# Second layer in f16 pairs instead of fp32r, scaled per tile from the energy of its tokens

## The chip, the core and the metric

The kernel runs on one core of one Trainium2 chip. The core has five engines with a queue of their own each: TensorE (PE, the matrix engine; PEld is its loading of the stationary matrix), VectorE (DVE), ScalarE (ACT), GpSimd (POOL) and SyncE (SP, which issues the transfers). The metric is the device time of one execution in microseconds; lower is better.

## What is computed

The input x has 8 batches of 3072 tokens with 256 numbers. Two layers follow a Fourier transform:

```python
X = np.fft.fft(np.fft.fft(x, axis=1), axis=2).real       # x: 8 x 3072 x 256
h = np.maximum(np.maximum(X @ w1, X @ w2), X @ w3)       # 256 -> 768
y = h @ w_out                                            # 768 -> 256, first layer's output
h = y @ w_in                                             # 256 -> 1024, second layer
e = np.exp(h - h.max(-1)); sm = e / (e.sum(-1) + 1e-09)
solu = h * sm
ln = (solu - mean(solu)) / np.sqrt(var(solu) + 1e-06) * g_ln
out = ln @ w_out2                                        # 1024 -> 256
```

The weights of the matrices come as f64 words and are decoded on the chip.

## The kernel before, in words

The work is cut into 48 tiles of 512 tokens, six for each batch. Precision comes from pairs: a number is held as a high and a low part, and a product of two such matrices is three matmuls (high by high, high by low, low by high). Everywhere but in the second layer's first product the parts are f16, brought into range by factors of two.

A batch begins with its loads (`x_load`, line 331), butterflies on POOL (`x_fly`, line 364), the split into f16 parts (`x_norm`, `x_hi`, `x_lo`, the tile `uh`), and the first half of the transform (`alpha_mm`, line 393). The stretch of the program in which a batch's 192 alpha matmuls lie between the tiles of the batch before it is called the alpha stretch below; there are seven of them inside the stream. A transpose by DMA gives `z` (`z_tr`), and `beta_mm` (line 428) finishes the transform for one tile, as the pair `pq`.

For each tile, the first layer takes 14 products `l1_mm` (line 529, two of them with `w3l`), each evacuated by ACT (`l1_b`, line 301) and DVE (`l1_n`, `l1_c`, lines 549, 562 and 563), six `relu` (line 568), six splits (`r_hi` on ACT, `r_lo` on POOL, lines 572 and 577) and six `m_mm` (line 587). `m_add` (DVE, line 591) gives the layer's output in two halves of 128 x 512. ACT rounds each half to fp32r (`mo_hi`, line 596) and POOL takes the rest (`mo_lo`, line 600); the pair `mo` is the second layer's input.

The second layer goes by four blocks of 128 tokens to a tile. `h_mm` (line 649) is 12 matmuls of 512 columns with blocks of `mo` as the stationary and the fp32r pair `win` as the moving matrix, in a PSUM tile `h` of which there is one. DVE takes the maximum (`h_max`, line 658) and three small operations on one column (`h_q`, lines 661 to 664), ACT the exponential (`h_exp`, line 671), DVE the product `v` (`h_v`, line 677), which frees `h`. ACT squares `v` (line 682) and rounds it to f16 (`v_hi`, line 704), POOL does small column operations (lines 687 to 699) and the low part (`v_lo`, line 708), the pair is transposed by DMA, and `o_mm` (line 722) is 24 matmuls of 256 columns.

The order on every engine is fixed when the program is built: a list scheduler (`Schedule.run`) keeps a model of each engine's clock from written durations, and takes on each engine the operation whose rank is lowest. The rank rests on a due time in tiles, to which a table of numbers, `BIAS`, adds by kind of operation. `CAPACITY` says how many buffers a pool has. Two PSUM banks (`misc`) are shared by alpha, beta, `o_mm` and the small sums over partitions (`spread`, line 320, a fp32 matmul with a 128 x 128 matrix of ones as the stationary, which stands in the trace as two matmul records).

Of the kernel before, what the change touches and what calls it, by code (L numbers as in the profile page):

```python
# [1158 lines left out]
```

## Time and profile before

| | |
|---|---|
| median of 3 runs | 2186.63 us (2185.48 to 2187.26) |
| profiled execution | 2187.91 us, of which its span, from the first to the last instruction, is 2186.1 us |
| mean granted TensorE clock | 0.983 of full speed |
| busy share of the span | PE 94%, PEld 72%, DVE 85%, ACT 65%, POOL 66% |
| the chain that ended last | PE 75%, DVE 11%, issue 4%, ACT 4%, POOL 3%, DMA 2% |
| of it, by line | h L649 21%, omm L722 19%, l L529 17%, m L587 14% |

Busy time is the time in which an engine had an instruction in work. The chain is followed back from the last instruction, at each step to what released it. A share over the whole span is an average of stretches with different limits.

### The profile page before, as it was taken

To read this page: it belongs to the slowest core of one execution; us is meant where nothing else is said; L and a number is where in the kernel's file an instruction comes from. 1 tells how busy PE (TensorE), PEld (TensorE's weight loads), DVE (VectorE), ACT (ScalarE), POOL (GpSimd) and SP (SyncE) were. 2 spreads that over 40 slices of the span, in tenths; PEclk is the share of its full clock that TensorE was granted. 3 is DMA by queue.
4 is the path that set the end of the run, shared out by engine and by line. 5 is a ranking of instruction groups with operands and counts; after the bars stand their busy time and mean duration, and the time that the engine had idled before them with its cause. 6 is when DMAs were issued, how large, how long until landed. Compare 5 with 4: busy or idle time off the path is not lost.

```text
span 2186.1 us, 44046 instructions
## 1 busy us (share of the span) xinstructions
PE 2044.8 (94%) x16130; PEld 1575.9 (72%) x16130; DVE 1849.0 (85%) x3993; ACT 1430.0 (65%) x2680; POOL 1434.7 (66%) x1688
## 2 busy tenths in 40 slices
PE   3568999999999999999999999999999999999998
PEld 2445777777777777777777777777777777777776
DVE  7978888888888888987898888988899888888884
ACT  2656765686657865677666776668666786666655
POOL 3657855686657855588566876579556885555653
PEclk8689999999999999999999999999999999999999
DMA  8352344744456344744348344553437543443324
GB/s 249 117 114 55 82 78 88 159 83 83 83 116 136 73 86 79 157 101 77 73 80 167 88 83 83 117 130 78 92 59 163 108 78 74 77 84 75 71 59 106
DMA packets 532617, 216.61 MB, mean 99 GB/s; under 512 B 504368, under 2 KB 504496, under 8 KB 532272
## 3 DMA queue, kind: packets, MB, share of 16 engines
q1 hardware_dynamic: 532400, 213.80, 47.0%
q8 instruction: 126, 2.06, 0.4%
q14 instruction: 91, 0.75, 0.1%
HBM read 62.76 MB, written 25.17 MB: 40 GB/s over the span
## 4 chain that ended last, share of the span: by engine, by line
PE 75%; DVE 11%; issue 4%; ACT 4%; POOL 3%; DMA 2%; SPq 0%; POOLq 0%; ACTq 0%; DVEq 0%
PE h L649 21%; PE omm L722 19%; PE l L529 17%; PE m L587 14%; PE alpha L393 2%; PE beta L428 1%; DVE sv L568 1%; DVE l L549 1%; DVE v L677 1%; POOL rhl L577 1%; DMA vt<-vh 1%; POOL mo L600 1%; POOL vh L708 1%; ACT bs L301 1%; DMA xa<-in_x_dram 1%
## 5 line engine op out<-in xcount | busy, mean ns | idle before, releaser
L649 PE MATMUL h<-win,mo 128*128 128x512 f32 x2280 | 577.5, 402 | 7.9 <-DVE v L677 7.9
L722 PE MATMUL omm<-wf,vt 128*128 128x256 f16 x4608 | 535.8, 273 | 11.4 <-DVE x L406 4.4
L722 PEld LDWEIGHTS <-vt 128*128 128x128 f16 x4608 | 450.5, 98 | 88.4 <-issue 10.0
L649 PEld LDWEIGHTS h<-win,mo 128*128 128x128 f32 x2280 | 418.4, 189 | 97.8 <-PE l L529 5.3
L529 PE MATMUL l<-pq,wl 128*128 128x256 f16 (+2 forms) x3456 | 455.8, 273 | 30.0 <-DVE sv L568 11.5
L708 POOL TENSOR_TENSOR vh<-v,vh 128x1024 f16<-128x1024 f32 x188 | 403.1, 2144 | 63.8 <-ACT vh L704 59.4
L549 DVE SCALAR_TENSOR_TENSOR l<-ny,wn,l 128x256 f32<-128x256 f32 (+1 forms) x672 | 322.5, 484 | 144.4 <-ACT bs L301 136.4
L577 POOL TENSOR_TENSOR rhl<-sv,rhl 128x512 f16<-128x512 f32 x288 | 335.7, 1169 | 161.2 <-ACT rhl L572 159.8
L587 PE MATMUL m<-rhl,wo 128*128 128x512 f16 x1728 | 415.7, 379 | 15.0 <-DVE s L591 10.6
L529 PEld LDWEIGHTS <-wl 128*128 128x128 f16 x3456 | 321.7, 97 | 130.3 <-issue 45.9
L301 ACT ACTIVATE bs<-l 128x256 f32<-128x256 f32 (+1 forms) x576 | 216.1, 381 | 161.3 <-PE l L529 157.1
L682 ACT ACTIVATE jk<-v,hst 128x1024 f16<-128x1024 f32 x192 | 220.1, 1147 | 144.9 <-DVE v L677 144.7
L658 DVE TENSOR_REDUCE hst<-h 128x1 f32<-128x1024 f32 x190 | 232.0, 1221 | 74.5 <-PE h L649 72.9
L587 PEld LDWEIGHTS <-wo 128*128 128x128 f16 x1728 | 163.9, 98 | 167.5 <-DVE s L591 11.3
L572 ACT CAST rhl<-sv 128x512 f16<-128x512 f32 x288 | 177.3, 616 | 152.2 <-DVE sv L568 136.1
L677 DVE SCALAR_TENSOR_TENSOR v<-h,hst,e 128x1024 f32<-128x1024 f32 x190 | 242.7, 1278 | 7.2 <-ACT e L671 5.0
L671 ACT ACTIVATE e<-h,hst 128x1024 f32<-128x1024 f32 x190 | 211.6, 1114 | 54.5 <-DVE hst L658 52.1
L695 POOL TENSOR_SCALAR hst<-hst,sc 128x1 f32<-128x1 f32 x192 | 66.0, 344 | 219.4 <-ACT jk L682 190.9
L704 ACT CAST vh<-v 128x1024 f16<-128x1024 f32 x192 | 200.0, 1042 | 4.2 <-DMA vt<-vh 2.7
L364 POOL TENSOR_TENSOR uv<-xs 96x512 f32<-96x512 f32 x128 | 167.7, 1334 | 32.9 <-DMA xs<-in_x_dram 25.3
L568 DVE SCALAR_TENSOR_TENSOR sv<-l,sv 128x512 f32<-128x512 f32 x240 | 164.8, 687 | 2.9
L600 POOL TENSOR_TENSOR mo<-s,mo 128x512 fp32r<-128x512 f32 x96 | 123.2, 1292 | 54.8 <-ACT mo L596 54.3
(148 smaller groups left out, 2558.9 us busy)
## 6 DMA issues: line engine op xcount, KB each, us to landing
xs<-in_x_dram SPq DMA_DIRECT2D x120, 384.0 KB, 4.1
out_dram<-ob SPq DMA_DIRECT2D x96, 256.0 KB, 2.9
raw<-in_w_dram SPq DMA_DIRECT2D x6, 768.0 KB, 5.3
raw<-in_w_out_dram SPq DMA_DIRECT2D x14, 256.0 KB, 2.9
xa<-in_x_dram SPq DMA_DIRECT2D x8, 384.0 KB, 7.9
vt<-vh SPq DMA_TRANSPOSE x192, 4.3
raw<-in_w_in_dram SPq DMA_DIRECT2D x4, 512.0 KB, 3.8
cb<-in_c_beta_dram SPq DMA_DIRECT2D x1, 1536.5 KB, 10.8
```

Source lines behind the costliest of these rows:

```text
L301: act.activation(dst, src, AF.Copy, scale=scale)
L529: mm(o, w_[w], hl[:, a, e, c0:c0 + n_], start=(n == 0), stop=(n == 2))
L549: dve.scalar_tensor_tensor(p[:, 0:WA], pq[s][1][:, 0:WA], w, p[:, 0:WA], ALU.mult, ALU.add)
L577: pool.tensor_tensor(t[:, 1], svs.pop((s, j, 0)), t[:, 0], ALU.subtract)
L587: mm(m[:, h], wo[:, w, j, hs], t[:, a], start=(j == 0 and n == 0), stop=(j == NJF - 1 and n == 2))
L649: mm(hp[:, f], m[:, a, d, ts_], win[:, w, d, fs], start=(n == 0), stop=(n == 5))
L658: dve.tensor_reduce(st[:, 0], y["h"], op=ALU.max, axis=AX.XY, negate=True)
L671: act.activation(y["e"], y["h"], AF.Exp, bias=st[:, 0], scale=1.0, accum_out=st[:, 3])
L677: dve.scalar_tensor_tensor(y["v"], y["h"], st[:, 2], y["e"], ALU.mult, ALU.mult, accum_out=st[:, 4])
L682: act.activation(new(hpool[0], "jk", [128, 2, 512], F16), y["v"], AF.Square, bias=st[:, 4], scale=-float(FF2), accum_out=st[:, 6])
L708: engine.tensor_tensor(y["vh"][:, 1], y["v"].rearrange("p a b -> p (a b)"), y["vh"][:, 0], ALU.subtract)
L722: mm(y["o"][:, 0:D], vt[:, a * 8 + c], wf[:, w, c], start=(n == 0), stop=(n == 23))
```

## The change

The second layer's input and its first matrix become f16 pairs. For that the values must be brought into f16's range, which the change does by a scale for each tile, taken from the energy of the tile's tokens: ACT squares the high half of `z` and sums it (`z_square`), one fp32 matmul of one column sums over the partitions (`z_total`), three small DVE operations make a power of two and its reciprocal (`z_least`, `z_root`, `z_recip`), and four on POOL give the scales that later steps take as a column (`z_unit`, `z_true`, `z_eps`). `mo_hi` becomes two ACT operations for each half: the f16 high part, and that part scaled back to f32 in a tile `mw`, from which POOL takes the low part. `win` holds three parts (high, low, and the high part scaled by 2**-11 for the product with the low part of `mo`), and its loading phase measures its maximum, scales it and splits it. `h_exp` scales the negated maximum by an ACT operation on one column and then scales inside the exponential; the first small operation of `h_q` takes a column in place of the number 1.0. All numbers of `BIAS` are new, several written durations too, `xa` has three buffers instead of four and `wi` four instead of one.

```diff
-CAPACITY = dict(l1=2, m=1, h=1, misc=2, xs=2, uv=2, uh=2, z=2, pq=2, bs=3, sv=3, sw=1, s2=2, rhl=3, mo=2, hst=4, e=1, v=2,
-                vh=2, vt=3, ob=2, xb=2, dg=1, raw=2, xa=4, wr=3, wi=1)
+CAPACITY = dict(l1=2, m=1, h=1, misc=2, xs=2, uv=2, uh=2, z=2, pq=2, bs=3, sv=3, sw=1, s2=2, rhl=3, mo=2, hst=4, ms=5, mw=2, e=1, v=2,
+                vh=2, vt=3, ob=2, xb=2, dg=1, raw=2, xa=3, wr=3, wi=4)
 X_POOL = ((0, 1, 0, 1, 0, 1, 0, 1), (1, 1, 1, 1, 1, 1, 1, 1))
...
-BIAS = {("ah", 0): -35.57, ("ah", 1): -76.89, ("al", 0): -26.93, ("al", 1): -159.58, ("alo", 0): -2.02,
+BIAS = {("xla", 0): -199.12, ("xmax", 0): -74.211, ("xld", 0): 91.084, ("xfly", 0): 125.294, ("xhs", 0): 51.043,
...
-    win = wp.tile([128, 2, 2, FF2], F32R, name="win")
+    win = wp.tile([128, 3, 2, FF2], F16, name="win")
...
-    def m_unit(b):
-        dve.tensor_scalar(xbt[b][:, 12:13], xbt[b][:, 10:11], sc[:, SC_M:SC_M + 1], 4.0, ALU.mult, ALU.mult)
+    m_unit = [
+        (130, lambda b: dve.tensor_scalar(xbt[b][:, 12:13], xbt[b][:, 10:11], sc[:, SC_M:SC_M + 1], 4.0, ALU.mult, ALU.mult)),
+        (130, lambda b: dve.tensor_scalar(xbt[b][:, 12:13], xbt[b][:, 12:13], am[:, 23:24], None, ALU.mult)),
+        (78, lambda b: dve.reciprocal(xbt[b][:, 13:14], xbt[b][:, 12:13])),
+    ]
...
+    mst, msp = {}, {}
+    MS_V, MS_R, MS_U, MS_T, MS_I, MS_E, MS_S = range(7)
+    def ms_col(s, c):
+        return mst[s][:, c:c + 1]
+    def z_square(s):
+        mst[s] = new(lp, "ms", [128, 8], F32)
+        act.activation(new(fp, "zj", [128, 8, 128], F16), zt[s][:, 0:8], AF.Square, scale=2.0**-8, accum_out=ms_col(s, MS_S))
+    def z_total(s):
+        msp[s] = misc("total")
+        mm(msp[s][:, 0:1], unit, ms_col(s, MS_S))
+    def z_least(s):
+        dve.tensor_scalar(ms_col(s, MS_V), msp.pop(s)[:, 0:1], 2.0**-20, None, ALU.max)
+    def z_root(s):
+        v = ms_col(s, MS_V).bitcast(I32)
+        dve.tensor_scalar(v, v, 1, 0x7F800000, ALU.logical_shift_right, ALU.bitwise_and)
+    def z_recip(s):
+        dve.reciprocal(ms_col(s, MS_R), ms_col(s, MS_V))
+    def z_unit(s):
+        pool.tensor_scalar(ms_col(s, MS_U), ms_col(s, MS_R), 2.0**-32, 2.0**-33, ALU.mult, ALU.mult)
+    def z_true(s):
+        t = xbt[s // NSB]
+        pool.tensor_scalar(ms_col(s, MS_T), ms_col(s, MS_V), t[:, 12:13], 2.0**76, ALU.mult, ALU.mult)
+        pool.tensor_scalar(ms_col(s, MS_I), ms_col(s, MS_R), t[:, 13:14], 2.0**-76, ALU.mult, ALU.mult)
+    def z_eps(s):
+        pool.tensor_scalar(ms_col(s, MS_E), ms_col(s, MS_I), sc[:, SC_E:SC_E + 1], ms_col(s, MS_I), ALU.mult, ALU.mult)
...
-            op(("be", *k), "PE", (360, 720)[p], beta_mm, k, v, deps=[("zt", s), ("constb",), *before], take=["misc"],
-               give=["z"] if p else [])
-            op(("bh", *k), "ACT", (264, 530)[p], beta_hi, k, v, deps=[("be", *k)] + [("bh", s, 0)] * p,
-               take=[] if p else ["pq"])
+            op(("be", *k), "PE", (360, 720)[p], beta_mm, k, v, deps=[("zt", s), ("constb",), *before],
+               take=["misc"] if p else ["misc", "pq"])
+            op(("bh", *k), "ACT", (264, 530)[p], beta_hi, k, v, deps=[("be", *k)] + [("bh", s, 0)] * p)
             op(("bl", *k), "DVE", 350, beta_lo, k, v, deps=[("bh", *k)], give=["misc"])
+        op(("zs", s), "ACT", 1135, z_square, (s,), v, deps=[("zt", s)], take=["ms"])
+        op(("zr", s), "ACT", 0, lambda s: zt.pop(s), (s,), v, deps=[("zs", s), ("be", s, 1)], give=["z"])
+        op(("ze", s), "PE", 120, z_total, (s,), v, deps=[("zs", s)], take=["misc"])
+        sch.chain(("zv", s), "DVE", [(130, z_least), (130, z_root), (78, z_recip)], (s,), v, deps=[("ze", s)], give=["misc"])
+        op(("zu", s), "Pool", 330, z_unit, (s,), v, deps=[("zv", s)])
+        op(("zm", s), "Pool", 760, z_true, (s,), v + 0.5, deps=[("zv", s), ("mu", b)])
+        op(("zq", s), "Pool", 390, z_eps, (s,), v + 1, deps=[("zm", s), ("wfc",)])
...
-        return 2.0**-21 if i < 2 else xbt[s // NSB][:, 12:13]
+        return 2.0**-21 if i < 2 else ms_col(s, MS_U)
...
-            mo[s] = new(hpool[0], "mo", [128, 2, 2, 512], F32R)
-        act.copy(mo[s][:, 0, h], svs[s, h, 2])
+            mo[s] = new(hpool[0], "mo", [128, 2, 2, 512], F16)
+        split_hi(mo[s][:, 0, h], svs[s, h, 2], 2.0**-11)
+        mw[s, h] = new(hpool[0], "mw", [128, 512], F32)
+        split_hi(mw[s, h], mo[s][:, 0, h], 2.0**11)
     def mo_lo(s, h):
         t = mo[s]
-        pool.tensor_tensor(t[:, 1, h], svs.pop((s, h, 2)), t[:, 0, h].bitcast(F32), ALU.subtract)
+        pool.tensor_tensor(t[:, 1, h], svs.pop((s, h, 2)), mw.pop((s, h)), ALU.subtract)
...
-               give=["m", "pq"] + (["xb"] if is_special(s) else []) if h else [])
-            op(("mh", *k), "ACT", 520, mo_hi, k, v, deps=[("ma", *k), ("open",)] + [("mh", s, 0)] * h,
-               take=[] if h else ["mo"])
-            op(("ml", *k), "Pool", 1225, mo_lo, k, v, deps=[("mh", *k)], give=["s2"])
+               give=["m", "pq"] if h else [])
+            op(("mh", *k), "ACT", 1050, mo_hi, k, v, deps=[("ma", *k), ("open",)] + [("mh", s, 0)] * h,
+               take=["mw"] if h else ["mo", "mw"])
+            op(("ml", *k), "Pool", 1225, mo_lo, k, v, deps=[("mh", *k)], give=["s2", "mw"])
...
-                for a, w in ((0, 0), (0, 1), (1, 0)):
+                for a, w in ((0, 0), (0, 1), (1, 2)):
...
-        (72, lambda s, t: dve.tensor_scalar(hx[s, t]["st"][:, 1], hx[s, t]["st"][:, 0], -1.0, 1.0, ALU.mult, ALU.max)),
+        (72, lambda s, t: dve.tensor_scalar(hx[s, t]["st"][:, 1], hx[s, t]["st"][:, 0], -1.0, ms_col(s, MS_I),
+                                           ALU.mult, ALU.max)),
...
-        act.activation(y["e"], y["h"], AF.Exp, bias=st[:, 0], scale=1.0, accum_out=st[:, 3])
+        act.activation(st[:, 11], st[:, 0], AF.Copy, scale=ms_col(s, MS_T))
+        act.activation(y["e"], y["h"], AF.Exp, bias=st[:, 11], scale=ms_col(s, MS_T), accum_out=st[:, 3])
...
-        pool.tensor_scalar(st[:, 8], st[:, 7], sc[:, SC_E:SC_E + 1], st[:, 7], ALU.mult, ALU.mult)
+        pool.tensor_scalar(st[:, 8], st[:, 7], ms_col(s, MS_E), st[:, 7], ALU.mult, ALU.mult)
...
-            sch.chain(("hk", *k), "DVE", h_q, k, v, deps=[("hm", *k)])
-            op(("he", *k), "ACT", 1095, h_exp, k, v, deps=[("hm", *k)], take=["e"])
+            sch.chain(("hk", *k), "DVE", h_q, k, v, deps=[("hm", *k), ("zm", s)])
+            op(("he", *k), "ACT", 1320, h_exp, k, v, deps=[("hm", *k), ("zm", s)], take=["e"])
...
-            sch.chain(("hs", *k), "Pool", [(200, h_g), (270, h_g2), (270, h_var)], k, v + 0.2, deps=[("hq", *k), ("wf",)])
+            sch.chain(("hs", *k), "Pool", [(320, h_g), (390, h_g2), (390, h_var)], k, v + 0.2, deps=[("hq", *k), ("zq", s)])
             if t % 2:
-                op(("hf", s, t // 2), "Pool", 640, h_pow, (s, t // 2), v, deps=[("hs", s, t - 1), ("hs", s, t)])
+                op(("hf", s, t // 2), "Pool", 640, h_pow, (s, t // 2), v, deps=[("hs", s, u) for u in range(t + 1)],
+                   give=["ms"] + (["xb"] if is_special(s) else []) if t == 3 else [])
...
+    def win_norm(h, f):
+        split_hi(tmp["i", h, f], tmp["i", h, f], sc[:, SC_I:SC_I + 1])
     def win_hi(h, f):
-        act.copy(win[:, 0, h, f * 512:(f + 1) * 512], tmp["i", h, f])
+        fs = slice(f * 512, (f + 1) * 512)
+        act.copy(win[:, 0, h, fs], tmp["i", h, f])
+        split_hi(win[:, 2, h, fs], win[:, 0, h, fs], 2.0**-11)
     def win_lo(h, f):
         fs = slice(f * 512, (f + 1) * 512)
-        pool.tensor_tensor(win[:, 1, h, fs], tmp.pop(("i", h, f)), win[:, 0, h, fs].bitcast(F32), ALU.subtract)
+        pool.tensor_tensor(win[:, 1, h, fs], tmp.pop(("i", h, f)), win[:, 0, h, fs], ALU.subtract)
+    def win_join():
+        dve.tensor_reduce(am[:, 22:23], am[:, 24:28], op=ALU.max, axis=AX.X)
     for h in range(2):
         for f in range(2):
             k = ("i", h, f)
             v = -0.3 + 0.1 * (2 * h + f)
             from_f64(k, [w_in2[h * 128:(h + 1) * 128, f * 512:(f + 1) * 512]], wi_dst(k), 512, v, take=["wi"])
-            pop(("wih", h, f), "ACT", 520, win_hi, (h, f), v, deps=[("gd", *k)])
+            pop(("ami", h, f), "ACT", 620, bound, (24 + 2 * h + f, lambda k=k: tmp[k], win[:, 0, h, f * 512:(f + 1) * 512]), v,
+                deps=[("gd", *k)])
+            pop(("wio", h, f), "ACT", 520, win_norm, (h, f), v, deps=[("isc",)])
+            pop(("wih", h, f), "ACT", 1000, win_hi, (h, f), v, deps=[("wio", h, f)])
             pop(("wil", h, f), "Pool", 1225, win_lo, (h, f), v, deps=[("wih", h, f)], give=["wi"])
+    pop(("amij",), "DVE", 80, win_join, (), 0.0, deps=[("ami", h, f) for h in range(2) for f in range(2)])
+    pow2_scale("is", 22, 1, [("amij",)], 0.0)
+    pop(("isc",), "DVE", 135, lambda: recip(SC_I, 23), (), 0.0, deps=[("is", "pow")])
```

The order of instructions, as the built programs have it, at three places.

On PE, in the stream, the end of a block of `h_mm` before; `wl` is the first layer's matrix, `l` its PSUM tile, and an fp32r matmul stands without a weight load of its own in this listing:

```order
L529 LDWEIGHTS wl_74
L529 MATMUL l_13754<-pq,wl_74 128x256
L649 MATMUL h<-win,mo 128x512 x12
L529 LDWEIGHTS wl_74
L529 MATMUL l_13789<-pq,wl_74 128x256
```

and now:

```order
L692 LDWEIGHTS mo
L692 MATMUL h<-win,mo 128x512
L570 LDWEIGHTS wl_74
L570 MATMUL l_7172<-pq,wl_74 128x255
L570 LDWEIGHTS wl_74
```

The block of twelve matmuls stands among the same neighbours as before; its form is that of the f16 products. The added sum over partitions stands once for each of the 48 tiles between such blocks:

```order
L570 LDWEIGHTS wl_74
L570 MATMUL l_7182<-pq,wl_74 128x257
L425 MATMUL total<-ms,unit 128x1
L628 LDWEIGHTS wo
L628 MATMUL m<-rhl,wo 128x512
```

On ACT, around the second layer's input of one tile, before (`bs` is the first layer's evacuation, `ob` the output's, `e`, `jk` and `vh` are the exponential, the square and the rounding of a block, `x` an evacuation of alpha):

```order
L301 ACTIVATE bs<-l_9456 128x256
L301 ACTIVATE bs<-l_9467 128x256
L671 ACTIVATE e,hst<-h,hst 128x1024
L596 CAST mo<-s_9020 128x512
L596 CAST mo<-s_9157 128x512
L729 ACTIVATE ob<-omm,hst 128x256
L402 CAST x_85<-alpha 128x6x16x4
L682 ACTIVATE jk,hst<-v,hst 128x1024
L704 CAST vh<-v 128x1024
```

and now, at a tile's input in the same part of the stream:

```order
L297 ACTIVATE bs<-l_9702 128x256
L715 ACTIVATE hst<-hst,ms 128x1
L716 ACTIVATE e,hst<-h,hst,ms 128x1024
L613 CAST rhl<-sv 128x512
L297 ACTIVATE mo<-s_9277 128x512
L297 ACTIVATE mw<-mo 128x512
L774 ACTIVATE ob<-omm,hst 128x256
L727 ACTIVATE jk,hst<-v,hst 128x1024
L297 ACTIVATE mo<-s_9405 128x512
L297 ACTIVATE mw<-mo 128x512
```

Each half of the input now takes two ACT operations, and each exponential has an operation on one column ahead of it.

On POOL, where a tile's scales are made, now (`ms` is the tile's column of scales, `bs` two cleared columns):

```order
L438 TENSOR_SCALAR ms<-ms 128x1
L442 TENSOR_SCALAR ms<-ms,xb 128x1
L443 TENSOR_SCALAR ms<-ms,xb 128x1
L446 TENSOR_SCALAR ms<-ms,sc 128x1
L732 TENSOR_SCALAR hst<-hst 128x1
L736 TENSOR_SCALAR hst<-hst,ms 128x1
```

The first four are new. Counted in the same listing from the last `vh` of one tile to the last `vh` of the second tile after it, in an alpha stretch, POOL has before 14 `uv`, 7 `uh`, 13 `rhl`, 4 `mo` and 8 `vh`; now it has 16 `uv`, 7 `uh`, 12 `rhl`, 4 `mo`, 8 `vh` and 8 `ms`.

## Rows read from the trace of the kernel before

**Rows 1.** The page: span, and busy time, share and instructions by engine.

```profile
span 2186.1 us, 44046 instructions
...
PE 2044.8 (94%) x16130; PEld 1575.9 (72%) x16130; DVE 1849.0 (85%) x3993; ACT 1430.0 (65%) x2680; POOL 1434.7 (66%) x1688
```

**Rows 2.** Busy time by stretch: opening, ramp, stream, end; then clock and DMA.

```profile
0.00:123.00 123.00, 56.78 (x371) 43.66 (x372) 98.64 (x137) 56.70 (x94) 58.31 (x42) 0.77 0.62 180
123.00:200.00 77.00, 56.92 (x396) 38.78 (x394) 59.79 (x137) 43.66 (x81) 47.84 (x44) 0.90 0.41 86
200.00:2150.00 1950.00, 1903.44 (x15185) 1471.57 (x15184) 1674.02 (x3692) 1313.52 (x2481) 1321.21 (x1588) 1.00 0.47 94
2150.00:2186.00 36.00, 27.66 (x187) 21.85 (x185) 16.59 (x28) 16.07 (x27) 7.38 (x15) 0.95 0.47 103
```

**Rows 3.** Waits of PE from 200 us: total us, times, longest.

```profile
PE m L587 <- DVE s L591: 10.6, 6, 1.8
...
PE alpha L393 <- DVE pq L304: 0.6, 1, 0.6
```

**Rows 4.** Timeline of PE: start, length, operation and count.

```profile
1009.79 3.01 PE L649 MATMUL h<-win,mo 128*128 128x512 f32 x12
1012.64 1.49 PE L529 MATMUL l<-pq,wl 128*128 128x256 f16 x12
...
1034.05 2.75 PE L587 MATMUL m<-rhl,wo 128*128 128x512 f16 x12
1036.64 0.82 PE L529 MATMUL l<-pq,w3l 128*128 128x256 f16 x6
```

**Rows 5.** Groups by line and shape on PE: busy us, mean ns, idle before.

```profile
L649 PE MATMUL h<-win,mo 128*128 128x512 f32 x2280 | 577.5, 402 | 7.9 <-DVE v L677 7.9
...
L649 PEld LDWEIGHTS h<-win,mo 128*128 128x128 f32 x2280 | 418.4, 189 | 97.8 <-PE l L529 5.3 <-issue 4.9
L587 PE MATMUL m<-rhl,wo 128*128 128x512 f16 x1728 | 415.7, 379 | 15.0 <-DVE s L591 10.6 <-POOL rhl L577 4.4
```

**Rows 6.** Timeline of PE around a fp32 sum over partitions.

```profile
413.77 0.39 PE L320 MATMUL spread<-dg,unit 128*128 128x128 f32 x2
413.99 0.82 PE L529 MATMUL l<-pq,wl 128*128 128x256 f16 x6
```

**Rows 7.** The same groups on DVE, small operations.

```profile
L662 DVE TENSOR_SCALAR hst<-hst 128x1 f32<-128x1 f32 x192 | 39.5, 206 | 0.9
...
L664 DVE RECIPROCAL hst<-hst 128x1 f32<-128x1 f32 x192 | 30.1, 157 | 2.5
...
L661 DVE TENSOR_SCALAR hst<-hst 128x1 f32<-128x1 f32 x192 | 28.5, 149 | 0.7
```

**Rows 8.** On ACT.

```profile
L682 ACT ACTIVATE jk<-v,hst 128x1024 f16<-128x1024 f32 x192 | 220.1, 1147 | 144.9 <-DVE v L677 144.7
...
L596 ACT CAST mo<-s 128x512 fp32r<-128x512 f32 x96 | 58.3, 614 | 19.8 <-DVE s L591 19.7
...
L682 ACT ACTIVATION_READ_ACCUMULATOR jk<-v,hst 128x1 f32 x192 | 36.2, 188 | 0.0
...
L853 ACT COPY wn<-prep 128x6 f32<-128x6 f32 x2 | 0.3, 138 | 0.0
```

**Rows 9.** On POOL.

```profile
L577 POOL TENSOR_TENSOR rhl<-sv,rhl 128x512 f16<-128x512 f32 x288 | 335.7, 1169 | 161.2 <-ACT rhl L572 159.8
...
L364 POOL TENSOR_TENSOR uv<-xs 96x512 f32<-96x512 f32 x128 | 167.7, 1334 | 32.9 <-DMA xs<-in_x_dram 25.3 <-DVE uh L304 4.4 <-ACT uh L372 2.3
...
L600 POOL TENSOR_TENSOR mo<-s,mo 128x512 fp32r<-128x512 f32 x96 | 123.2, 1292 | 54.8 <-ACT mo L596 54.3
...
L691 POOL TENSOR_SCALAR hst<-hst,sc 128x1 f32<-128x1 f32 x192 | 68.0, 354 | 19.2
```

**Rows 10.** Two tiles of an alpha stretch, cut at the last vh of each.

```profile
1194.50:1235.80 41.30, 41.30 (x335) 31.75 (x334) 34.57 (x80) 30.63 (x57) 33.62 (x35) 1.00 0.49 106
1235.80:1283.00 47.20, 45.57 (x440) 36.48 (x440) 41.40 (x91) 39.42 (x70) 45.37 (x41) 1.00 0.33 74
```

More of the change, by code (lines that the diff above doesn't have):

```diff
@@ L291, in fft_moe_solu_kernel @@
     x1 = fp.tile([128, NSB, 4, 4, 128], F16, name="x1")
-    SC_W, SC_O, SC_3, SC_F, SC_M, SC_E, SC_V = 0, 1, 2, 3, 8, 9, 10
+    SC_W, SC_O, SC_3, SC_F, SC_I, SC_M, SC_E, SC_V = 0, 1, 2, 3, 4, 8, 9, 10
     def at_least(dst, src, scale=2.0**-13):
@@ L439, in beta_mm @@
             run(WB, 1, 0, 0, lambda t: t[:, 0:1].broadcast_to([128, 128]))
-            zt.pop(s)
         bps[s, part] = p
@@ L466, in fft_moe_solu_kernel @@
             buf = "xs" if b else "xa"
-            op(("xla", *k), "SP", 1090, x_load, k if b else (*k, tp, "xa"), v - 0.5,
+            op(("xla", *k), "SP", 1450, x_load, k if b else (*k, tp, "xa"), v - 0.5,
                deps=[("xla", b, c - 1)] if c else [("xld", b - 1, NCH - 1)] if b else [], take=[buf] if c else [buf, "xb"], lag=2500)
@@ L473, in fft_moe_solu_kernel @@
             v = max(NSB * b - 1.8, -1.0) + 0.09 * c
-            op(("xld", *k), "SP", 1090, x_load, k, v - 0.5, deps=[("xld", b, c - 1)] if c else [("xla", b, NCH - 1)] if b else [], take=["xs"],
+            op(("xld", *k), "SP", 1450, x_load, k, v - 0.5, deps=[("xld", b, c - 1)] if c else [("xla", b, NCH - 1)] if b else [], take=["xs"],
                lag=2500)
@@ L495, in fft_moe_solu_kernel @@
         sch.chain(("xsc", b), "DVE", x_scale, (b,), v, deps=[("xall", b)], give=["misc"])
-        op(("mu", b), "DVE", 130, m_unit, (b,), v + 0.3, deps=[("xsc", b), ("scm",)])
+        sch.chain(("mu", b), "DVE", m_unit, (b,), v + 0.3, deps=[("xsc", b), ("scm",), ("isc",)])
     for s in range(NT):
@@ L506, in fft_moe_solu_kernel @@
             before = [("be", s, 0)] if p else [("be", s - 1, 1)] if s else []
-            op(("be", *k), "PE", (360, 720)[p], beta_mm, k, v, deps=[("zt", s), ("constb",), *before], take=["misc"],
-               give=["z"] if p else [])
-            op(("bh", *k), "ACT", (264, 530)[p], beta_hi, k, v, deps=[("be", *k)] + [("bh", s, 0)] * p,
-               take=[] if p else ["pq"])
+            op(("be", *k), "PE", (360, 720)[p], beta_mm, k, v, deps=[("zt", s), ("constb",), *before],
+               take=["misc"] if p else ["misc", "pq"])
+            op(("bh", *k), "ACT", (264, 530)[p], beta_hi, k, v, deps=[("be", *k)] + [("bh", s, 0)] * p)
             op(("bl", *k), "DVE", 350, beta_lo, k, v, deps=[("bh", *k)], give=["misc"])
-    l1s, svs, rs, rhl, mt, mts, mo = {}, {}, {}, {}, {}, {}, {}
+        op(("zs", s), "ACT", 1135, z_square, (s,), v, deps=[("zt", s)], take=["ms"])
[5 more added lines that the diff above has]
+        op(("zq", s), "Pool", 390, z_eps, (s,), v + 1, deps=[("zm", s), ("wfc",)])
+    l1s, svs, rs, rhl, mt, mts, mo, mw = {}, {}, {}, {}, {}, {}, {}, {}
     def l1_weights(i, j):
@@ L606, in l1_ops @@
         if stays(k[0], k[2]):
-            op(("l1c", *k), "DVE", 790, l1_c, k, v, deps=[("l1n", *k)], give=["bs"])
+            op(("l1c", *k), "DVE", 808, l1_c, k, v, deps=[("l1n", *k)], give=["bs"])
         else:
-            op(("l1c", *k), "DVE", 790, l1_c, k, v, deps=[("l1n", *k)], take=[sv_tag(k[2])], give=["bs", "l1"])
+            op(("l1c", *k), "DVE", 662 if k[2] < 2 else 790, l1_c, k, v, deps=[("l1n", *k)], take=[sv_tag(k[2])], give=["bs", "l1"])
     for s in range(NT):
@@ L617, in fft_moe_solu_kernel @@
             v = s + (2 * j + 1) / 12
-            op(("rl", *k), "DVE", 663, relu, k, v, deps=[("l1c", s, j, 1), ("l1c", s, j, 0)], give=["l1" if stays(s, 1) else "sw"])
+            op(("rl", *k), "DVE", 608, relu, k, v, deps=[("l1c", s, j, 1), ("l1c", s, j, 0)], give=["l1" if stays(s, 1) else "sw"])
             op(("rh", *k), "ACT", 520, r_hi, k, v, deps=[("rl", *k)], take=["rhl"])
@@ L624, in fft_moe_solu_kernel @@
             k = (s, h, 2)
-            l1_ops(k, s + (h + 4.5) / 6, [("w3l",), ("mu", s // NSB)])
+            l1_ops(k, s + (h + 4.5) / 6, [("w3l",), ("zu", s)])
             k = (s, h)
@@ L817, in from_f64 @@
     def from_f64(key, srcs, dst, n, v, take=(), after=()):
-        pop(("ld", *key), "SP", 2.8 * n, f64_load, (key, srcs, n), v - 0.2, deps=after, take=["raw", *take], lag=2000)
+        pop(("ld", *key), "SP", 3.6 * n, f64_load, (key, srcs, n), v - 0.2, deps=after, take=["raw", *take], lag=2000)
         magnitude, parts = f64_parts(key, dst, n)
@@ L853, in w_evac_n @@
         act.copy(wn[:, i - 1], tmp.pop(("n", i))[:, 0:NJF])
-    am = tp.tile([128, 24], F32, name="am")
+    am = wp.tile([128, 28], F32, name="am")
     def amax(col, t):
```

51 lines of the change are left out of this document (24 added, 27 removed), and 57 rows, old and new, of the table BIAS.

## The prediction

> **What bounds the kernel now.** The page comes first: a span of 2186.1 us, PE busy for 2044.8 of it, DVE for 1849.0, ACT and POOL near 1430 [rows 1]. The busy share by stretch says where PE is not busy [rows 2]. In the opening (to 123 us) and the ramp (to 200 us) it idles for 86.3 us; in the stream, from 200 to 2150 us, it is busy for 1903.44 of 1950 us at a granted clock of 1.00, its upper level of 2.4 GHz; the end leaves 8.3 us idle. So in nine tenths of the time PE lacks 46.6 us to being full. What it still waits for is nearly all DVE: the waits of PE after 200 us hold ten lines with DVE as the releaser, from 10.6 us down to 0.6 us [rows 3], together 41.4 us (10.6 + 6.4 + 4.8 + 4.4 + 4.2 + 3.8 + 2.7 + 2.0 + 1.9 + 0.6). Time taken off PE's instructions in the stream is time off the kernel, as far as DVE, ACT and POOL can follow; they are busy there for 86%, 67% and 68%.
>
> **The block h_mm.** In the timeline one block of twelve fp32r matmuls starts at 1009.79 us and its successor at 1012.64: 2.85 us, 237 ns for each matmul. Twelve f16 matmuls of the same 512 columns, `m_mm`, start at 1034.05 and are followed at 1036.64: 2.59 us, 216 ns each [rows 4]. The lengths of single records agree: 402 ns against 379 [rows 5], and 23 ns by the 2304 matmuls (192 blocks of twelve) is 53 us. The form changes, the number and the columns don't. I take the timeline: 192 x 0.26 = 49.9 us less on PE, with 53 us as the other end. The rows show one thing that goes with the longer step: an fp32r weight load lasts 189 ns [rows 5].
>
> The Trainium skill ("TensorE: Matmul & The Clock Gate", section "Back-to-back issue gap") gives a gap at the full clock that depends on the columns alone, about 216 ns for 512. The f16 row meets that and the fp32r row is 21 ns above it; if the rule held for fp32r too, this term would be zero and the sum below 2208 us. The measurement decides here, and the term stays.
>
> **The sum over partitions.** 48 fp32 matmuls of one column come in, each two records. The nearest row is a `spread` of 128 columns in the stream: it starts at 413.77 us and the next matmul at 413.99 [rows 6], 0.22 us with its weight loads. 48 x 0.22 = 10.6 us on PE. Fewer columns can only make it cheaper, but the weight loads remain, so 5 to 11 us; I take 10.6. It waits for `z_square` on ACT, which needs only the transposed `z`, as the beta matmuls do. It also holds one of the two `misc` banks until three small DVE operations are through; alpha, beta and `o_mm` are queued for these banks. That goes into the waits below.
>
> **DVE.** In `h_q` a number becomes a column. The operation with a number takes 149 ns, the one with a column 206 [rows 7]: 192 x 57 ns = 10.9 us. The chain of a tile is three operations like 149 to 206, 149 and 157 ns, about 0.49 us, 23.5 us for 48. Together 34 us, of which the stream gets some 33. None of it lies on PE's path by itself; it takes DVE's slack. DVE is free for 276 of 1950 us now, 14.1%. Afterwards it has 1674 + 33 = 1707 us of work in 1950 - 49.9 + 10.6 + 11 = 1922 us, 11.2% free. I let PE's 41.4 us of waits for DVE grow as this free share falls: 41.4 x (14.1 / 11.2) = 52, **11 us more**. That is a choice; its bounds are 20 us less (the table of priorities is new and may order the stream better: half of the present waits gone) and 40 us more (PE's idle time in the stream nearly doubled).
>
> **ACT.** Each tile gets `z_square`, like the square of 128 x 1024 with its read of the sum, 1147 + 188 ns; two more operations of 128 x 512, 614 ns each; and four operations on one column, of which the nearest rows are 138 ns and, as the upper end, 188 [rows 8]. That is 1.34 + 1.23 + about 0.7 = 3.3 us a tile, 157 us in all. ACT goes from 67% of the stream to about 76%. It hides as long as the order leaves room. On the way of one block, `h` is held 0.14 to 0.19 us longer by the new operation before the exponential, and its matmuls give back 0.26; on the way from `m_add` to the next tile's first block there is 0.61 us more, covered by first-layer matmuls that stand between.
>
> **POOL.** Four column operations a tile like 354 ns [rows 9], 1.4 us; `mo_lo` now writes f16, as `rhl` does, 1169 ns instead of 1292, 0.25 us back. Net 1.2 us a tile, 55 us in all; 68% becomes 71% on average, but not evenly (third rival).
>
> **Opening and ramp.** `win` gets a longer preparation: four maxima, a sum over partitions, four scalings and four extra f16 parts on ACT, some 8 us by the 614 ns row, while ACT is busy for 100 of the first 200 us [rows 2]. The work before the first beta on DVE is the same but for two maxima of x that move behind it; eight matmuls of `w_out2`'s mean move from before the first beta to behind it. I take zero, with 6 us gained and 12 lost as bounds. The end keeps its shape: four output blocks after the last `h` before, five now.
>
> **The sum.** 2186.1 - 49.9 + 10.6 + 11 = 2157.8 us of span. The profiled execution took 1.8 us more than its span, and the median of the runs is 1.3 us below that execution, so I predict a median of **2158 us**, 1.3% less.
>
> **Rivals.**
> *The waits shrink.* The written durations now lie nearer to what the trace shows; a block of `h_mm` was written as 2600 ns and took 2850, and now takes what is written. If half of the stream's 46.6 us goes, the sum is 2158 - 11 - 23 = 2124. For it: PE's waits are short and many, as from an order that is slightly off. Against it: three engines have more to do.
>
> *The other engines take most of it back.* ACT at 76% and DVE at 89% on average means stretches that are full. If PE's idle time in the stream rises from 46.6 to 80 us instead of 58, the time is 2180.
>
> *POOL sets the pace of the alpha stretches: slower.* Two tiles of one such stretch take 88.5 us, in which POOL is busy for 79.0 [rows 10], 89%. By the counts of the listing the same span of program has 2 `uv` more (2.7 us), one `rhl` less (1.2), 8 `ms` (2.8) and four shorter `mo` (0.5 less): 82.8 us. At 89% that is 92.7 us, where the forecast needs 88.5 - 1.6 = 86.9; 5.8 us in each of seven stretches is 41 us, and the time 2199. For it: the first layer's splits and the second layer's low parts stand in the same queue. Against it: the second of the two tiles already runs at 45.37 of 47.20 us, 96%, and in the view from which [rows 3] come no line has PE waiting for POOL. It decides from 4.1 us a stretch, that is if POOL cannot pass 91% there.
>
> *The f16 block is no shorter than the fp32r block.* The time would be 2158 + 49.9 = 2208. The gap by columns alone that the Trainium skill states (same page and section) is the rule by which it would come out so. Against it stands the row of `m_mm`, with the same shape in the same clock. It decides from a block of about 2.74 us.
>
> **How the numbers follow.** A measurement of this kernel can tell about 0.2%, 4.4 us, from no change, so faster begins below 2182 us. The forecast, 2143 to 2170, has a chance of 0.50; shrinking waits, below 2143, 0.17; the engines taking back most, 2170 to 2182, 0.15, and all of it, 2182 to 2191, 0.07; POOL's pace 0.08 and no shorter block 0.03, above. Faster 0.82, same 0.07, slower 0.11. The range of 8 in 10 runs from 2130 to 2184; the forecast's own is 2143 to 2170.
>
> **What would show it.** Right: blocks of h at 2.59 us between starts, weight loads well under 189 ns, `total` at 0.22 us or less, PE idle in the stream between 40 and 75 us, the first block of h near 164 us as before. Wrong: PE waits for POOL or ACT with more than 20 us in all, two tiles of an alpha stretch above 91 us with POOL over 90% busy, a first block of h later than 176 us, or lines in which PE waits for a `misc` bank that the scale's chain holds.

## The result, and the profile after

The changed kernel takes 2126.11 us (median of 4 runs, 2124.19 to 2126.63), against 2186.46 for the kernel before beside it: a ratio of 0.9723, interval 0.9706 to 0.9739. That is 60 us less, where 28 were forecast, and just under the stated range. Its profiled execution has a span of 2124.3 us, 61.8 less.

The page: span, then busy time, share and instructions by engine (to [rows 1]).

```profile
span 2124.3 us, 44538 instructions
...
PE 2011.5 (95%) x16228; PEld 1399.4 (66%) x16228; DVE 1850.2 (87%) x4158; ACT 1602.2 (75%) x3081; POOL 1470.8 (69%) x1880
```

Busy time by stretch, in the columns of [rows 2].

```profile
0.00:123.00 123.00, 57.55 (x374) 44.94 (x375) 97.68 (x142) 60.27 (x104) 46.52 (x38) 0.72 0.62 181
123.00:200.00 77.00, 64.01 (x429) 41.07 (x426) 65.51 (x170) 58.08 (x113) 60.38 (x67) 0.92 0.35 75
200.00:2090.00 1890.00, 1862.02 (x15216) 1291.92 (x15215) 1671.79 (x3825) 1466.94 (x2838) 1358.48 (x1762) 1.00 0.48 98
2090.00:2124.30 34.30, 27.88 (x217) 21.45 (x215) 15.27 (x24) 16.90 (x31) 5.40 (x15) 0.95 0.53 108
```

PE's waits from 200 us (to [rows 3]), whole.

```profile
PE l L570 <- DVE sv L609: 8.3, 10, 0.9
PE l L570 <- DVE sw L604: 6.9, 7, 1.4
PE h L692 <- DVE v L722: 5.9, 14, 0.8
PE l L570 <- DVE sv L604: 2.9, 8, 0.7
PE l L570 <- DVE s L604: 2.9, 5, 1.1
PE omm L767 <- DMA vt<-vh: 2.8, 1, 2.8
PE omm L767 <- DVE pq L300: 0.7, 2, 0.4
PE m L628 <- DVE s L632: 0.2, 1, 0.2
```

The 61.8 us are 33.3 of PE's busy time and 28.5 of its idle time. In the stream PE is idle for 28.0 us instead of 46.6, and in the ramp for 13.0 instead of 20.1. The lines with DVE as releaser, seven now, sum to 27.8 us instead of 41.4; the largest of before, `m` waiting for `m_add` with 10.6 us, is down to 0.2, though DVE is busier than before: 88.5% of the stream, against 85.8%. Of POOL and ACT as releasers there is no line (ACT had 5.1 us before, in three lines).

The blocks of matmuls in question, by line and shape (to [rows 5]), and the sum over partitions.

```profile
L692 PE MATMUL h<-win,mo 128*128 128x512 f16 x2280 | 523.3, 379 | 7.0 <-DVE v L722 7.0
L692 PEld LDWEIGHTS <-mo 128*128 128x128 f16 x2304 | 222.4, 98 | 252.3 <-DVE v L722 9.7 <-issue 3.7
L425 PE MATMUL total<-ms,unit 128*128 128x1 f32 x96 | 14.5, 220 | 0.8 <-ACT mean L1126 0.8
```

### The profile page after: what moved, and what is told of

It reads as the page before. It is cut to its first block, busy times and chain, and to the rows that moved or that the text cites. A ratio compares the mean times of both kernels' runs of the same rounds, so it can differ in the third digit from the quotient of the medians.

```text
span 2124.3 us, 44538 instructions
## 1 busy us (share of the span) xinstructions
PE 2011.5 (95%) x16228; PEld 1399.4 (66%) x16228; DVE 1850.2 (87%) x4158; ACT 1602.2 (75%) x3081; POOL 1470.8 (69%) x1880
## 4 chain that ended last, share of the span: by engine, by line
PE 61%; DVE 17%; ACT 6%; DMA 3%; issue 3%; POOL 2%; ACTq 0%; POOLq 0%; DVEq 0%
PE h L692 16%; PE omm L767 16%; PE l L570 13%; PE m L628 12%; DMA z<-x 3%; DVE v L722 3%; DVE l L590 3%; DVE sv L609 2%; DVE hst L701 2%; PE beta L464 2%; ACT bs L297 1%; ACT e L716 1%; POOL vh L753 1%; DVE l L604 1%; PE alpha L392 1%
## 5 line engine op out<-in xcount | busy, mean ns | idle before, releaser
L692 PE MATMUL h<-win,mo 128*128 128x512 f16 x2280 | 523.3, 379 | 7.0 <-DVE v L722 7.0
L570 PEld LDWEIGHTS <-wl 128*128 128x128 f16 x3456 | 331.7, 98 | 128.9 <-issue 14.8
L590 DVE SCALAR_TENSOR_TENSOR l<-ny,wn,l 128x256 f32<-128x256 f32 (+1 forms) x672 | 316.8, 482 | 105.6 <-ACT bs L297 104.2
L692 PEld LDWEIGHTS <-mo 128*128 128x128 f16 x2304 | 222.4, 98 | 252.3 <-DVE v L722 9.7
L716 ACT ACTIVATE e<-h,hst,ms 128x1024 f32<-128x1024 f32 x190 | 228.8, 1204 | 6.3
L613 ACT CAST rhl<-sv 128x512 f16<-128x512 f32 x288 | 176.6, 613 | 67.3 <-DVE sv L609 46.6
L376 POOL TENSOR_TENSOR uh<-uv,uh 96x1024 f16<-96x1024 f32 x60 | 127.8, 2132 | 14.0 <-ACT uh L371 12.8
```

The costliest lines, as they stand in the source:

```text
L570: mm(o, w_[w], hl[:, a, e, c0:c0 + n_], start=(n == 0), stop=(n == 2))
L590: dve.scalar_tensor_tensor(p[:, 0:WA], pq[s][1][:, 0:WA], w, p[:, 0:WA], ALU.mult, ALU.add)
L692: mm(hp[:, f], m[:, a, d, ts_], win[:, w, d, fs], start=(n == 0), stop=(n == 5))
L716: act.activation(y["e"], y["h"], AF.Exp, bias=st[:, 11], scale=ms_col(s, MS_T), accum_out=st[:, 3])
```

## The experiments

One theory says that the new order (the table and the corrected durations) took the waits away; its rival says that the f16 form did so. All runs are below; then each group. PE's idle time is that of its stream, from 200 us to 34 us before the end, and DVE's share is of the same stretch.

| kernel | median us | ratio to before | PE idle us | DVE busy |
|---|---|---|---|---|
| before | 2186 | 1 | 46.6 | 85.8% |
| changed | 2126.1 | 0.9723 (0.9706 to 0.9739) | 28.0 | 88.5% |
| form_only | 2152.0 | 0.9843 (0.983 to 0.9856) | 47.5 | 86.8% |
| form_undone | 2161.8 | 0.9884 (0.9869 to 0.99) | 20.6 | 87.2% |
| old_table | 2181.0 | 0.9979 (0.997 to 0.9987) | 50.2 | 86.1% |
| hybrid | 2175.5 | 0.9954 (0.994 to 0.9967) | 44.1 | 86.3% |
| a_old_hs | 2165.2 | 0.9902 (0.9888 to 0.9915) | 51.8 | 86.1% |
| a_m_1295 | 2159.1 | 0.9876 (0.9862 to 0.9889) | 45.2 | 86.4% |
| a_h_2590 | 2157.2 | 0.9864 (0.9849 to 0.9879) | 50.0 | 87.3% |
| a_o_2610 | 2128.4 | 0.9736 (0.972 to 0.9753) | 24.8 | 87.8% |
| new_durs_before | 2155.8 | 0.986 (0.9847 to 0.9873) | 18.4 | 86.1% |
| b_hs | 2160.0 | 0.9875 (0.9862 to 0.9889) | 21.2 | 85.8% |
| b_dve | 2167.2 | 0.9912 (0.9899 to 0.9926) | 30.0 | 84.8% |
| b_o_2610 | 2176.4 | 0.9955 (0.9943 to 0.9968) | 37.6 | 85.4% |
| b_h_2700 | 2180.4 | 0.997 (0.9959 to 0.9982) | 35.1 | 84.7% |
| b_m_1295 | 2188.8 | 1.0011 (1.0002 to 1.002) | 46.9 | 86.3% |
| form_and_durs | 2117.7 | 0.9688 (0.9674 to 0.9701) | 17.4 | 87.4% |
| no_total | 2118.1 | 0.9689 (0.9675 to 0.9702) | 27.2 | 88.7% |
| act_light | 2122.9 | 0.9709 (0.9695 to 0.9722) | 28.3 | 88.6% |
| am_light | 2149.8 | 0.9836 (0.9822 to 0.985) | 41.0 | 86.7% |

**The form alone, in either order.** form_only puts it into the kernel before:

```diff
-    win = wp.tile([128, 2, 2, FF2], F32R, name="win")
+    win = wp.tile([128, 2, 2, FF2], F16, name="win")
...
-            mo[s] = new(hpool[0], "mo", [128, 2, 2, 512], F32R)
+            mo[s] = new(hpool[0], "mo", [128, 2, 2, 512], F16)
```

> The kernel before with the second layer's input and matrix as f16 pairs and nothing else: no scale, no added work, the order of every engine as before. (The values are not brought into f16's range, so the numbers that come out are not the reference's.) If the new order gave the unforeseen 30 us, this kernel gains the block of h alone: 2186 - 50 = 2136 us, within 6, with PE's waits in the stream near the 46.6 us of before. If the shorter f16 blocks themselves take waits away (earlier release of the banks, shorter weight loads), it comes to 2126 or below, with waits near 28 us.

form_undone takes it out of the changed kernel:

```diff
-    win = wp.tile([128, 3, 2, FF2], F16, name="win")
+    win = wp.tile([128, 1, 2, FF2], F32R, name="win"); winl = wp.tile([128, 2, FF2], F16, name="winl")
...
-            mo[s] = new(hpool[0], "mo", [128, 2, 2, 512], F16)
+            mo[s] = new(hpool[0], "mo", [128, 2, 2, 512], F32R)
...
-                for a, w in ((0, 0), (0, 1), (1, 2)):
+                for a, w in ((0, 0), (0, 0), (1, 0)):
```

> The changed kernel with the pair and the matrix back in fp32r, all its added work and its order on every engine kept. (All three products take the high part of the matrix, for want of room, so the result is less exact.) If the order gave the unforeseen part: 2126 + 50 = 2176 us, within 5, PE's waits in the stream still near 28 us. If the form gave it: 2186 or above, with waits back at 46 us or more.

The form is worth 34.0 us in the old order and 35.7 in the new, and changes PE's idle time by +0.9 and +7.4: it takes no waits away. Neither theory had the size, which both took from the prediction's 49.9. (The inputs of this case leave the pair inside f16's range without the scale, other than the expectation said.) Where the other 15 us are, the same place of the program shows: a block of `m`, one of `h`, the next of `l`. PE's timeline (start, length, operation, count) of the changed kernel, in f16:

```profile
1204.56 1.46 PE L628 MATMUL m<-rhl,wo 128*128 128x512 f16 x6
1205.85 2.75 PE L692 MATMUL h<-win,mo 128*128 128x512 f16 x12
1208.44 0.82 PE L570 MATMUL l<-pq,w3l 128*128 128x256 f16 x6
```

And of form_undone, in fp32r:

```profile
1219.69 1.46 PE L628 MATMUL m<-rhl,wo 128*128 128x512 f16 x6
1220.80 3.13 PE L692 MATMUL h<-win,mo 128*128 128x512 f32 x12
1223.77 0.83 PE L570 MATMUL l<-pq,w3l 128*128 128x256 f16 x6
```

From `h` to `l` it is 2.59 against 2.97 us. But the fp32r block is recorded as starting 1.11 us after the start of `m`, the f16 block 1.29: from `m` to `l`, 3.88 against 4.08 us, the difference is 0.20. Start to start, an fp32r block shows some of the time of the block ahead of it as its own.

**The order.** old_table keeps all the work of the change and puts back `BIAS` of before; hybrid adds to that the new entries of the kinds of operation that only the changed kernel has:

```diff
-BIAS = {("xla", 0): -199.12, ("xmax", 0): -74.211, ("xld", 0): 91.084, ("xfly", 0): 125.294, ("xhs", 0): 51.043,
+BIAS = {("ah", 0): -35.57, ("ah", 1): -76.89, ("al", 0): -26.93, ("al", 1): -159.58, ("alo", 0): -2.02,
```

> The changed kernel with the table of priorities of before (new kinds of operation get none), its written durations kept. If the table orders the stream better, the 18.6 us of the stream and some of the 7 of the ramp come back, and the added work costs waits as the prediction had it: 2150 us or above. If the form or the corrected durations took the waits away, it stays within 5 us of 2126.

> The changed kernel with the table of before for the kinds of operation that both kernels have, and the new table's entries for the new kinds (the sum, the scale, the loading phase of the matrix). If the run with the old table was slow only because the new kinds had no priority: 2140 us or below. If the table has to fit as a whole: 2165 us or above.

55 and 49 us of the gain go: entries for the new kinds are not enough. Not all of it is waiting in the stream. Of the 54.4 us that old_table's span is longer, 22 are idle time of PE in the stream, 13 are its idle time in the ramp and at the end, and 19 are busy time; in the ramp its granted clock is 0.81, against 0.92 in the changed kernel. new_durs_before does the opposite, with the kernel before:

```diff
-            op(("l1c", *k), "DVE", 790, l1_c, k, v, deps=[("l1n", *k)], give=["bs"])
+            op(("l1c", *k), "DVE", 808, l1_c, k, v, deps=[("l1n", *k)], give=["bs"])
...
-            op(("rl", *k), "DVE", 663, relu, k, v, deps=[("l1c", s, j, 1), ("l1c", s, j, 0)], give=["l1" if stays(s, 1) else "sw"])
+            op(("rl", *k), "DVE", 608, relu, k, v, deps=[("l1c", s, j, 1), ("l1c", s, j, 0)], give=["l1" if stays(s, 1) else "sw"])
...
-            sch.chain(("hs", *k), "Pool", [(200, h_g), (270, h_g2), (270, h_var)], k, v + 0.2, deps=[("hq", *k), ("wf",)])
+            sch.chain(("hs", *k), "Pool", [(320, h_g), (390, h_g2), (390, h_var)], k, v + 0.2, deps=[("hq", *k), ("wf",)])
```

> The kernel before with the written durations of the change where both have the operation (loads, first layer's evacuation, relu, small POOL operations) and the bank pair pq taken earlier, its table kept. If the corrected durations are what shortens PE's waits: 2170 us or below. If the table does it, which was fitted to the old durations here: between 2180 and 2200.

Not shown are `l1_c` at 662 where the result leaves its bank, longer written durations of the loads, and the buffers of `pq` taken by the first beta matmuls instead of by the ACT operation behind them. The new numbers lie nearer to the trace of the kernel before. Here are the three POOL operations of `hs` and the next one, from POOL's timeline:

```profile
1012.32 0.27 POOL L687 TENSOR_SCALAR hst<-hst 128x1 f32<-128x1 f32 x1
1012.69 0.34 POOL L691 TENSOR_SCALAR hst<-hst,sc 128x1 f32<-128x1 f32 x1
1013.13 0.34 POOL L695 TENSOR_SCALAR hst<-hst,sc 128x1 f32<-128x1 f32 x1
1013.43 2.13 POOL L708 TENSOR_TENSOR vh<-v,vh 128x1024 f16<-128x1024 f32 x1
```

From the first start to the last it is 1.11 us, where 0.74 was written and 1.10 is now.

The kernel is 30 us faster with not one operation changed. Its waits of PE from 200 us, the first lines:

```profile
PE omm L722 <- DMA vt<-vh: 6.1, 3, 2.5
PE h L649 <- DVE v L677: 4.8, 6, 1.5
PE l L529 <- DVE sv L563: 4.6, 7, 1.5
PE l L529 <- DVE sv L568: 2.8, 5, 1.1
```

The wait of `m` for `m_add`, 10.6 us in [rows 3], has no line here. In a_old_hs it is back. That is the changed kernel with three written durations of before:

```diff
-            sch.chain(("hs", *k), "Pool", [(320, h_g), (390, h_g2), (390, h_var)], k, v + 0.2, deps=[("hq", *k), ("zq", s)])
+            sch.chain(("hs", *k), "Pool", [(200, h_g), (270, h_g2), (270, h_var)], k, v + 0.2, deps=[("hq", *k), ("zq", s)])
```

> The changed kernel with the written durations of the three small POOL operations as before (200, 270 and 270 ns, where the trace shows 346); all else, the table too, as changed. It moves the order without any change of work. If the table of priorities is sharply fitted to its durations, this costs 10 us or more: 2136 or above. If only true durations that matter on PE's path count, it stays within 5 us of 2126.

```profile
PE h L692 <- DVE v L722: 10.7, 14, 2.0
PE m L628 <- DVE s L632: 9.5, 4, 2.4
PE l L570 <- DVE sv L604: 8.2, 10, 1.4
```

These are the first lines of the same view for a_old_hs. It costs 39 us. Is it the wrong durations, or would any other order cost as much? a_m_1295, a_o_2610 and a_h_2590 disturb the changed kernel by a duration that is as true as before:

```diff
-            op(("m", *k), "PE", 1300, m_mm, k, s + (j + 1.7) / 6,
+            op(("m", *k), "PE", 1295, m_mm, k, s + (j + 1.7) / 6,
...
-            op(("o", *k), "PE", 2620, o_mm, k, v, deps=[("vt", *k), ("wf",)], take=["misc"], give=["vt"])
+            op(("o", *k), "PE", 2610, o_mm, k, v, deps=[("vt", *k), ("wf",)], take=["misc"], give=["vt"])
...
-            op(("h", *k), "PE", 2600, h_mm, k, v, deps=[("ml", s, 0), ("ml", s, 1), ("win",)] + ([("h", s, t - 1)] if t else []),
+            op(("h", *k), "PE", 2590, h_mm, k, v, deps=[("ml", s, 0), ("ml", s, 1), ("win",)] + ([("h", s, t - 1)] if t else []),
```

> The changed kernel with one written duration moved by 0.4%: the six matmuls of m_mm as 1295 ns instead of 1300, both within what the trace shows (1.29 to 1.30 us). It moves about as many rows of PE's order as the run with the old POOL durations (13,268 of 32,039 against 13,704). If a true duration is what counts and wrong POOL durations cost the 39 us, it stays within 6 us of 2126. If the table fits one order only and any other order of this kernel is worse, it comes to 2140 or above.

> The changed kernel with o_mm written as 2610 ns instead of 2620, as in the second control on the kernel before (10 us faster there). If the new table fits one order and a disturbed one loses what the fit gave: 2145 or above. If the loss with m_mm at 1295 was a chance of that one order: within 8 us of 2126.

> The changed kernel with the block of h written as 2590 ns instead of 2600, which is what the trace shows. Fitted order: 2145 or above. Chance: within 8 us of 2126.

33, 2 and 31 us slower. So it takes no false duration to lose half of the gain, and none of the six other orders of this kernel is faster than the one that its table gives. The stream of a_m_1295, in the columns of [rows 2]:

```profile
200.00:2122.00 1922.00, 1876.85 (x15263) 1298.15 (x15262) 1661.29 (x3824) 1468.87 (x2838) 1359.29 (x1761) 1.00 0.47 96
```

With the same instructions as the changed kernel PE is idle for 45.2 us, and over the span 2022.4 us busy, 10.9 more. Busy time hides part of a stop: a record of 512 columns is 379 ns long and its successor can start 216 ns after it, so that a stop of less than 163 ns leaves no gap between records, and a longer one shows 163 ns less than it lasts. The view of PE's waits from 200 us has 69 waits here and 48 in the changed kernel.

On the kernel before, b_hs and b_dve make the corrections one by one; b_m_1295 and b_o_2610 are controls, and b_h_2700 corrects the block of `h`. The edits are of the lines shown (b_hs: `hs`; b_dve: `l1c`, also to 662 where it does not stay in its bank, and `rl`; the others 1300 to 1295, 2620 to 2610, 2600 to 2700).

> The kernel before with only the three small POOL durations corrected (320, 390 and 390 ns written instead of 200, 270 and 270). If these are what made the order of before bad: 2165 us or below, most of the 30 us of all corrections. If the durations of DVE (or chance) did it: within 8 us of 2186.

> The kernel before with only the DVE durations corrected (evacuation of the first layer 808 and 662 ns instead of 790, relu 608 instead of 663). PE's waits there are waits for DVE, so if true durations count these should: 2165 us or below. If the gain of all corrections was a lucky order, this run can fall on either side, 2170 to 2210.

> The kernel before with one written duration moved by 0.4% (m_mm 1295 ns instead of 1300), nothing corrected. If the corrections of POOL and DVE durations gained 26 and 19 us because they were corrections, this run stays within 8 us of 2186. If the order of before was simply a poor one, so that nearly any other order is better, it comes to 2175 or below.

> The kernel before with another written duration moved by 0.4% (o_mm 2610 ns instead of 2620), a second control. Within 8 us of 2186 if only corrections help; 2175 or below if the order of before was a poor one; above 2194 if it was a fitted one.

> The kernel before with the fp32r block of h written as 2700 ns instead of 2600, near what the trace shows net of its overlap with the block ahead (2.85 less 0.08 to 0.19 us). If the wrong duration of this block made the order of before poor: 2165 us or below. If not: within 8 us of 2186, or wherever chance puts it.

The corrections of POOL and DVE gain 27 and 19 us, the controls lose 2 and gain 10, and the correction of the block of `h`, on PE itself, gains 6. That the corrections help because they are true is not shown: two controls are few, and the gains do not add up (27 + 19 = 46 us one by one, 30 in new_durs_before, which makes both and more). The loads' durations and the earlier `pq` were not tried alone. What is shown is that the old table held no special order: of six disturbances one is slower, by 2 us.

**The added work.** no_total leaves out the matmul, and act_light the ACT operations that follow the scale; am_light is act_light in the order of a_m_1295.

```diff
-        mm(msp[s][:, 0:1], unit, ms_col(s, MS_S))
+        pass
...
-    dve.tensor_scalar(ms_col(s, MS_V), msp.pop(s)[:, 0:1], 2.0**-20, None, ALU.max)
+    msp.pop(s); dve.tensor_scalar(ms_col(s, MS_V), ms_col(s, MS_S), 2.0**-20, None, ALU.max)
```

> The changed kernel without the matmul that sums over the partitions; the scale comes from each partition's own sum (so the sum over partitions is left out), everything else stands in the same order. If it costs only its own time on PE: 48 x 0.14 to 0.24 us, so 2126 - 7 to 12 = 2114 to 2119. If the bank that it holds or its wait for the square costs more: 2110 or below. If it falls into waits anyway: 2122 or above.

```diff
-        mw[s, h] = new(hpool[0], "mw", [128, 512], F32)
-        split_hi(mw[s, h], mo[s][:, 0, h], 2.0**11)
+        mw[s, h] = mo[s][:, 0, h]
...
-        act.activation(st[:, 11], st[:, 0], AF.Copy, scale=ms_col(s, MS_T))
-        act.activation(y["e"], y["h"], AF.Exp, bias=st[:, 11], scale=ms_col(s, MS_T), accum_out=st[:, 3])
+        act.activation(y["e"], y["h"], AF.Exp, bias=st[:, 0], scale=1.0, accum_out=st[:, 3])
```

> The changed kernel with the ACT additions left out that follow the scale: the second operation of the rounding, the one on one column before the exponential, and the scale inside the exponential (so the scale is not applied there). About 134 us less work on ACT, the order of all else kept. If ACT's work is hidden, as the prediction had it: within 5 us of 2126. If ACT at 75% costs PE waits by holding h, bs or the pair mo longer: 2115 or below.

> The changed kernel in the order of the run with m_mm written as 1295 ns (2159 us there), with the same ACT additions left out as in the earlier light run (134 us of work; the scale is not applied there). If the added ACT work is hidden in any order: within 6 us of 2159. If it is hidden only in the fitted order: 2149 or below.

Leaving out the matmul gains 8.0 us: 48 times 0.14 is 6.7, by two lines of PE's timeline of the changed kernel, and little is left for its bank.

```profile
913.29 0.28 PE L425 MATMUL total<-ms,unit 128*128 128x1 f32 x2
913.43 2.78 PE L767 MATMUL omm<-wf,vt 128*128 128x256 f16 x24
```

The ACT work costs 3.2 us in the fitted order and 9.2 in the disturbed one: it is nearly hidden, and better hidden in the fitted order than in the one other order that was tried. ACT is busy for 111 us less in act_light, not 134, and POOL for 11 us less, since `mo_lo` then subtracts an f16 operand; the 3.2 us hold both.

**Both gains without the scale.** form_and_durs is new_durs_before with the two lines of form_only.

> The kernel before with both single parts at once: f16 pairs without a scale, and the corrected written durations with its own table. If the two gains (34 and 30 us) are independent, 2186 - 64 = 2122 us, within 6. If the shorter blocks and the corrected order take the same waits away, 2135 or above.

2117.7 us is faster than both kernels. The two gains add up (34.0 + 30.1, measured 68.8), so the form does not need the new table, and the table of before with the new durations does as well. It lacks the scale and all the work of it. The matmul of the scale alone is worth 8.0 us in no_total, as much as the 8.4 us between this kernel and the changed one, but the two stand in different orders.

## Why the prediction was wrong

- **The waits of PE** are the step that failed: "I let PE's 41.4 us of waits for DVE grow as this free share falls", plus 11 us. The order sets them, not DVE's free share (a_m_1295 changes nothing but the order), and the 28.0 us of idle stream lie below the 40 to 75 that were to show the forecast right. The changed kernel has DVE free for 11.5% and PE idle for 28.0 us; a_m_1295, with the same work, 13.6% and 45.2. With the form at -35 and the matmul at +8, the measured -60 leave -33 for order and added work together, where +11 stood. The bound of 20 us less was too near: halving the waits was the most that I allowed, while three written durations move the time by 39.
- **The rival "the waits shrink"**, at 2124, is what came, with a reason that fits the runs ("The written durations now lie nearer to what the trace shows"; that this gave the shorter waits is not shown) but at a chance of 0.17, and by errors that cancel: its block of `h` was 15 us too good, its waits 10 us not good enough.
- **The block h_mm**: right mechanism, mis-sized. Forecast 49.9 us, measured 34.0 and 35.7. One interval from start to start was multiplied by 192, and the overlap with the block ahead was not looked for. The rule of the Trainium skill for the gap of a single matmul ("TensorE: Matmul & The Clock Gate", section "Back-to-back issue gap"), 216 ns for 512 columns, fits the f16 block here too (2.59 us by 12); for fp32r it would have given no gain, and the measured 34.0 and 35.7 us decide against that.
- **The sum over partitions**: 10.6 forecast, 8.0 measured; PE's waits from 200 us have no line for it.
- **DVE**: the column operand takes 207 ns, as forecast, but busy time rose by 1.2 us only, not 34. The split of the special tiles (`relu`, from `sw`) fell from 1367 to 1079 ns, 13.8 us over 48, and the rest lies in small groups. POOL stands at 72% of the stream, near the forecast 71.
- **ACT**: 157 us forecast, 172 measured, 78% of the stream where 76 stood. The one-column operation was under-priced (0.14 to 0.19 us; it takes 293 ns), and the exponential grew from 1114 to 1204 ns. **POOL**: `mo_lo` did not get shorter.

```profile
L715 ACT ACTIVATE hst<-hst,ms 128x1 f32<-128x1 f32 x192 | 56.2, 293 | 39.1 <-DVE hst L701 37.9
L716 ACT ACTIVATE e<-h,hst,ms 128x1024 f32<-128x1024 f32 x190 | 228.8, 1204 | 6.3
...
L643 POOL TENSOR_TENSOR mo<-s,mw 128x512 f16<-128x512 f32 x96 | 123.5, 1295 | 12.2 <-ACT mw L297 11.8
```

These are groups of the changed kernel on ACT and POOL, as in [rows 8] and [rows 9].

- **POOL's pace in the alpha stretches**: did not come. One stretch of the changed kernel, in the columns of [rows 2]:

```profile
1213.00:1292.00 79.00, 78.23 (x743) 56.39 (x742) 68.53 (x157) 70.17 (x131) 75.32 (x75) 1.00 0.40 88
```

POOL is busy for 95% of it, more than the 91% from which the rival was to decide, and PE for 99%. The new order spreads a batch's alpha matmuls over 79 us where 42 to 48 were before, so that the stretch that [rows 10] measure no longer exists.
- **Opening and ramp**: forecast 0 within -6 and +12; the ramp has 7.1 us less idle time, though the first block of `h` starts at 168.9 us, between the two signs named (164 and 176).

What stays open is how the -33 us divide between table and durations, and why one order of the same work is better than another. The changed kernel with the old DVE durations was not tried.

## What to carry to other kernels

Where a list scheduler sets the order, a change that comes with new priorities or durations is two changes: price the order by its own spread, which is to be had from the kernel before by moving one written duration by half a per cent (here 2 to 10 us; 2, 31 and 33 in the fitted kernel), and do not derive waits from an engine's busy share. Measure what a block costs from the start of the block ahead of it to the start of the one behind it, over pairs of the same neighbours. Correct the written durations first: here that cost nothing and gained half of what the whole change did, though a duration moved from one value near the truth to another gained 10 us too.
